# A fused attention and mixture-of-experts kernel on one Trainium2 core: the first pairs' loads and transposes issued in another order, a table load moved forward, and scale and row-half steps moved in VectorE's order

## Chip, cores and metric

The kernel runs on one core of a Trainium2 chip. The metric is the device time of one execution in microseconds (us). A core has five engines with queues of their own: PE (TensorE, matrix products; its weight loads are listed as PEld), DVE (VectorE), ACT (ScalarE), POOL (GpSimd) and SP (SyncE, which here only issues DMAs). DMAs are issued by SP, ACT and POOL; the issuing is listed under SPq, ACTq and POOLq.

## What is computed

Attention over 4 batches, 8 heads, 576 positions, 64 dimensions, in which only scores within `tau` (0.02) of a row's maximum take part, and then a mixture of 8 experts of which each token uses one:

```python
scores = scale * q @ k.T                                   # per batch and head
thresh = max(scores, -1) - tau
scores = where(scores >= thresh, scores, -1e9)
attn   = exp(scores - max); attn /= sum(attn) + 1e-9
x      = (attn @ v), heads side by side                    # 2304 tokens x 512
logits = x @ w_gate; e = argmax(logits); gate = softmax(logits)[e]
# each expert takes at most `capacity` (576) tokens, in token order
h = relu(x[e's tokens] @ w1[e])                            # 512 -> 1024
y = h @ w2[e]                                              # 1024 -> 512
out[token] = gate * y                                      # 0 where not kept
```

All arrays are float32. The kernel splits each operand of a product into a float16 high half and a float16 low half and sums three products.

## The kernel before

**Attention.** The 32 (batch, head) problems are done as 16 pairs of two heads, four pairs to a batch. For pair s the kernel loads k and q (`load`, L730 for the main part, L733 for the two 64-row tails) and v (L728); loads of v for pairs 0 and 1 are issued by POOL. ACT writes the high half (`emit_hi`, L745), DVE the low half for pairs 0 and 1 (`emit_lo`, L754) and POOL that of the later pairs (L752). SP then issues a transposing DMA for k (`emit_turn_k`, L774) and one for q (`emit_turn_q`, L779). PE multiplies kT and qT into scores s (L792), DVE takes the maxima (L819 to L825) and forms from them an additional column block m (`emit_m`, L833 to L838), which a third transposing DMA turns (`emit_turn_m`, L784). PE then computes the differences d = s - max (L792 again, other operands), ACT exponentiates (L880), DVE keeps what is over the threshold (L884), ACT and POOL split p (L850, L854), PE multiplies with v (`av`, L900 and L912), DVE divides (L935), and the result goes through x, logits (L966, L981), gate (L1021 and on) and a scatter of token rows to a buffer `xd` in DRAM, sorted by expert.

**Mixture of experts.** Rows of `xd` are gathered in 21 tiles of 128 tokens: 8 early ones (one for each expert, gathered once three of the four batches are scattered) and 13 late ones (gathered after the last batch). For each tile PE transposes the rows (`x0`, L351), ACT writes the high half (`xh`, L354), DVE the low half (`xl`, L359), PE multiplies with w1 (`A`, L377 for early tiles, L384 for late ones), ACT and DVE make the hidden rows (L402, L406), late ones are transposed by a DMA (L412), PE multiplies with w2 (`B`, L423). The weights come in two chunks of F; their halves are made by ACT (L307, L309, L310), DVE (L314) and POOL (L312). `scales` (L430 and L433) reads two columns of gathered rows and makes the output row numbers `oix` and the factors `gsc`; it runs once for the early tiles and once for each group of 8 late tiles, so it waits until the last gather of its group has landed.

**What sets the order.** The program is not written in execution order. Each step is a task, `T(key, engine, duration, function, dependencies, priority)`, and the class `Plan` (L35 to L163) simulates the engines with a list scheduler: at each moment an engine takes, of the tasks whose dependencies are done, the one with the lowest priority number. The tasks are emitted in the order found, and the semaphore waits follow from the data. A dependency that is only in the plan changes the order on all engines but adds no wait by itself; an engine executes its list strictly in order. Priorities of attention tasks are 9 s plus an offset for each kind; those of early tiles were `NU + PR["early"]` plus 0.284 for each tile. `FIRST_A` (L1168) names the loads that ACT issues in place of SP: by (pair, is it q). The lines of the changed kernel are one higher than here after L706, and two higher behind L1418.

Names in the rows: `kr`, `qr` raw k and q; `kn`, `qn` their halves; `kT`, `qT` the transposed halves; `xd` the scattered rows; `earlyx`, `latex` halves of gathered rows; `earlyy`, `latey` the gathered rows and later the output tiles; `w1b`, `w2b` buffers with halves of weights (also used for d and p in attention); `gp`, `b`, `xo`, `s` are PSUM banks.

## Time and profile before

| what | us |
|---|---|
| runs of the kernel before | 628.80, 628.95, 637.29; median 628.95 |
| the profiled execution, its own time | 626.25 |
| its span in the profile | 624.4 |
| PE busy in it | 556.9 |

The profile is of one execution. Times in it run from the span's start. An idle time is put down to the one that released the engine. The granted clock (PEclk) is that of TensorE as a share of full speed.

### The profile page before, as it was taken

To read this page: it belongs to the slowest core of one execution; us is meant where nothing else is said; L and a number is where in the kernel's file an instruction comes from. 1 tells how busy PE (TensorE), PEld (TensorE's weight loads), DVE (VectorE), ACT (ScalarE), POOL (GpSimd) and SP (SyncE) were. 2 spreads that over 40 slices of the span, in tenths; PEclk is the share of its full clock that TensorE was granted. 3 is DMA by queue.
4 is the path that set the end of the run, shared out by engine and by line. 5 is a ranking of instruction groups with operands and counts; after the bars stand their busy time and mean duration, and the time that the engine had idled before them with its cause. 6 is when DMAs were issued, how large, how long until landed. Compare 5 with 4: busy or idle time off the path is not lost.

```text
span 624.4 us, 15985 instructions
## 1 busy us (share of the span) xinstructions
PE 556.9 (89%) x5990; PEld 378.3 (61%) x5990; DVE 432.3 (69%) x990; ACT 383.3 (61%) x523; POOL 426.9 (68%) x366
## 2 busy tenths in 40 slices
PE   0777999998999999999797895799999999999994
PEld 0234666765667666666566784665775577468652
DVE  4667988878886888886877869444555655555652
ACT  4359888878797688574467643448556645644410
POOL 5327887949887389772768536508788948886774
PEclk9989999989999899998798888989999999999997
DMA  5878777736677367662243845962579519861972
GB/s 152 193 174 166 135 149 138 152 95 156 152 171 137 58 172 133 116 87 49 77 141 99 296 160 157 223 157 77 203 194 220 173 67 222 207 202 61 232 185 100
DMA packets 171181, 94.26 MB, mean 151 GB/s; under 512 B 147027, under 2 KB 159383, under 8 KB 171098
## 3 DMA queue, kind: packets, MB, share of 16 engines
q1 hardware_dynamic: 157450, 50.47, 40.1%
q0 software_dynamic: 12352, 41.80, 20.8%
q8 instruction: 52, 0.85, 0.6%
q10 hardware_dynamic: 1296, 0.89, 0.4%
q14 instruction: 31, 0.25, 0.1%
HBM read 53.25 MB, written 10.24 MB: 102 GB/s over the span
## 4 chain that ended last, share of the span: by engine, by line
PE 60%; DVE 14%; DMA 9%; SPq 5%; ACT 4%; issue 4%; POOL 3%; ACTq 0%; POOLq 0%; DVEq 0%
PE b L384 10%; PE xo L900 9%; PE s L792 8%; PE d L792 7%; PE b L377 7%; PE xo L423 5%; PE gp L423 4%; PE b L423 4%; DVE w2b L884 3%; PE gp L966 2%; DMA out_dram<-latey,oix 2%; PE xo L912 2%; DVE mx L819 2%; SPq L733 2%; DMA qr<-in_q_dram 2%
## 5 line engine op out<-in xcount | busy, mean ns | idle before, releaser
L792 PE MATMUL s<-kT,qT 128*128 128x512 f16 (+2 forms) x576 | 99.5, 310 | 28.8 <-DMA kT<-kn 22.2
L819 DVE TENSOR_REDUCE mx<-s 128x1 f32<-128x512 f32 x144 | 94.4, 679 | 17.4 <-PE s L792 16.6
L792 PE MATMUL d<-qT,kT 128*128 128x512 f16 (+2 forms) x576 | 85.4, 302 | 6.0 <-DVE w2b L884 4.5
L384 PE MATMUL b<-w1b,latex 128*128 (+2 forms) x816 | 79.4, 274 | 5.3 <-DVE latex L359 3.6
L309 ACT ACTIVATE ws<-ws 128x1024 f32<-128x1024 f32 x48 | 50.5, 1051 | 51.1 <-DMA ws<-in_moe_w_dram 51.1
L384 PEld LDWEIGHTS <-latex 128*128 128x128 f16 (+1 forms) x816 | 62.3, 102 | 21.3 <-DVE latex L359 4.8
L792 PEld LDWEIGHTS <-qT 128*128 128x128 f16 (+1 forms) x640 | 39.7, 105 | 57.3 <-issue 25.7
L884 DVE SCALAR_TENSOR_TENSOR w2b<-d,ntau,w2b 128x1024 f32<-128x1024 f32 x56 | 71.0, 1276 | 3.6 <-ACT w2b L880 3.6
L854 POOL TENSOR_TENSOR p<-w2b,p 128x1024 f16<-128x1024 f32 x33 | 70.3, 2135 | 3.2 <-ACT p L850 2.8
L312 POOL TENSOR_TENSOR w2b<-ws,w2b 128x1024 f16<-128x1024 f32 x24 | 51.0, 2137 | 23.0 <-ACT w2b L310 22.8
L792 PEld LDWEIGHTS <-kT 128*128 128x128 f16 (+1 forms) x640 | 37.1, 102 | 47.7 <-issue 28.0
L312 POOL TENSOR_TENSOR w1b<-ws,w1b 128x1024 f16<-128x1024 f32 x24 | 51.3, 2141 | 20.6 <-ACT w1b L310 20.3
L880 ACT ACTIVATE w2b<-d 128x1024 f32<-128x1024 f32 x56 | 56.3, 1019 | 5.5 <-PE d L792 4.7
L900 PEld LDWEIGHTS <-p 128*128 128x128 f16 x1056 | 47.2, 103 | 14.8 <-issue 4.1
L377 PE MATMUL b<-earlyx,w1b 128*128 128x128 f16 x768 | 51.1, 228 | 5.4 <-DVE earlyx L359 5.2
L377 PEld LDWEIGHTS <-w1b 128*128 128x128 f16 x768 | 47.4, 102 | 12.8 <-issue 10.3
L900 PE MATMUL xo<-vH,p 128*128 128x65 f16 x704 | 49.9, 199 | 3.9 <-DVE rc L935 2.6
L423 PEld LDWEIGHTS <-lateh 128*128 128x128 f16 (+1 forms) x408 | 30.8, 103 | 33.6 <-issue 0.4
L296 POOL DMA_DIRECT2D ws<-in_moe_w_dram x50 | 37.3, 750 | 9.7 <-DVE w2b L314 7.3
L900 PE MATMUL xo<-vL,p 128*128 128x64 f16 x352 | 43.9, 197 | 0.0
L850 ACT ACTIVATE p<-w2b 128x1024 f16<-128x1024 f32 x33 | 34.8, 1055 | 6.1 <-DVE w2b L884 5.8
L310 ACT ACTIVATE w2b<-ws 128x1024 f16<-128x1024 f32 x24 | 25.4, 1057 | 20.9 <-PE gp L423 20.2
(231 smaller groups left out, 1225.6 us busy)
## 6 DMA issues: line engine op xcount, KB each, us to landing
ws<-in_moe_w_dram POOLq DMA_DIRECT2D x50, 512.0 KB, 5.1
ws<-in_moe_w_dram SPq DMA_DIRECT2D x14, 512.0 KB, 4.7
kr<-in_k_dram SPq DMA_DIRECT2D x15, 256.0 KB, 2.9
qr<-in_q_dram SPq DMA_DIRECT2D x14, 256.0 KB, 2.9
v<-in_v_dram SPq DMA_DIRECT2D x28, 128.0 KB, 3.2
qr<-in_q_dram ACTq DMA_DIRECT2D x2, 256.0 KB, 4.8
v<-in_v_dram POOLq DMA_DIRECT2D x4, 128.0 KB, 3.3
qT<-qn SPq DMA_TRANSPOSE x32, 4.7
```

Of the source, the lines that this page charges most:

```text
L296: eng.dma_start(out=t, in_=src)
L309: nc.scalar.activation(out=t, in_=t, func=AF.Copy, scale=W_SCALE)
L312: nc.gpsimd.tensor_tensor(out=dst[:, :, 1, :], in0=t, in1=dst[:, :, 0, :], op=ALU.subtract)
L377: nc.tensor.matmul(out=hp[:, f * P:(f + 1) * P], lhsT=wb[0][:, o:o + P], rhs=xT[t][:, xi], start=(d == 0 and z == 0), stop=(d == NB - 1 an ...
L384: nc.tensor.matmul(out=hp[m, 0:FC], lhsT=xT[t][:, xi, m], rhs=wb[0][:, bass.ds(r + (2 * d + wi) * FC, FC)], start=(d == 0 and z == 0), sto ...
L423: nc.tensor.matmul(out=yp[m], lhsT=h[:, o, hi, m], rhs=wb[1][:, bass.ds(r + wi * DM, DM)], start=(z == 0), stop=(z == len(ops) - 1),)
L792: nc.tensor.matmul(out=out, lhsT=l, rhs=r, start=(z == 0), stop=(z == 1), **kw)
L819: V.tensor_reduce(out=m[:, i, 0:1], in_=ps_s[i % 2], axis=AX.X, op=ALU.max)
L854: eng.tensor_tensor(out=p[:, 1], in0=p32_of(s, k), in1=p[:, 0], op=ALU.subtract)
L880: nc.scalar.activation(out=t, in_=d, func=AF.Exp, scale=sc_s)
L884: V.scalar_tensor_tensor(out=t, in0=d, scalar=ntau, in1=t, op0=ALU.is_ge, op1=ALU.mult)
L900: nc.tensor.matmul(out=ps_x[:, j * DV:j * DV + r.shape[-1]], lhsT=l, rhs=r, start=(z == 0), stop=(z == len(ops) - 1))
```

## The change

Seven edits, all in the planner's input or in what stands ahead of it:

1. A one-column `Exp` on ACT (L707 of the changed kernel) from the tile `ones`, ahead of everything else that ACT does. Before, ACT's one table load stands ahead of its first ACTIVATE (L745).
2. `FIRST_A` holds q of pair 0 only; q and k of pair 1 are issued by SP.
3. The loads of pair 2 depend on pair 0's transposes in the plan, those of pair 3 on pair 2's; the load of v for pair 2 depends on the transpose of k of pair 2.
4. The transposes of pair 2 depend on `tm` of pair 0, the transpose of its m block.
5. `scales` of a late group depends on the low half `xl` of the group's last tile too.
6. `scales` of the early tiles gets the priority `NU - 6` in place of `NU + PR["early"] + 20`.
7. `x1` and `x2` (`xh` and `xl`) of the early tiles get `NU - 9 + 0.284 t` in place of `NU + PR["early"] + 0.284 t`.

```diff
--- before.py
+++ after.py
@@ -704,6 +704,7 @@
         xss = [right.tile([P, NJ, D + 1], F32, name=f"xs{i}") for i in range(3)]
         rcs = [right.tile([P, 2, NJ, 1], F32, name=f"rc{i}") for i in range(3)]
 
+        nc.scalar.activation(out=cbuf[0][:, 0:1], in_=ones[:, 0:1], func=AF.Exp, scale=sc_s)
         for i in range(NKN):
             V.memset(kns[i][:, 1, :, D:], 0.0)
             V.memset(kns[i][:, 1, :, D:D + 1], MC)
@@ -1165,7 +1166,7 @@
 
         CUT = 2 * NJ + 3
         FIRST = 2
-        FIRST_A = {(0, True), (1, False), (1, True)}
+        FIRST_A = {(0, True)}
         BY_V = set()
         SI = list(range(2 * NJ)) + [2 * NJ, 2 * NJ + 1, 2 * NJ + 2]
         SD = [432] * (2 * NJ) + [560, 560, 180]
@@ -1177,7 +1178,7 @@
                 n = "q" if is_q else "k"
                 src, raws = (q, qraws) if is_q else (k, kraws)
                 eng, en, occ = (nc.scalar, "A", 460) if (s, is_q) in FIRST_A else (nc.sync, "S", 600)
-                T(("l" + n, s), en, 3 * occ, partial(load, src, raws[s % NRAW], s, eng), last("lo" + n, s - NRAW), u + PR["ld"] + is_q, dma=(728, 90, 90), kind="load")
+                T(("l" + n, s), en, 3 * occ, partial(load, src, raws[s % NRAW], s, eng), last("lo" + n, s - NRAW) + ([("tk", 0), ("tq", 0)] if s == 2 else [("tk", 2), ("tq", 2)] if s == 3 else []), u + PR["ld"] + is_q, dma=(728, 90, 90), kind="load")
                 nat = s - (NQN if is_q else NKN)
                 free = last("tm" if is_q else "tk", nat)
                 got = [("l" + n, s)] + ([("tau",)] if is_q and s == 0 else [])
@@ -1190,10 +1191,10 @@
                 T(("hi" + n, s), "A", 1170, partial(emit_hi, s, is_q, scaled), got + free, u + PR["hi"] + is_q)
                 T(("lo" + n, s), "G" if scaled else "V", 1270 if scaled else 760, partial(emit_lo, s, is_q, scaled), [("hi" + n, s)], u + PR["lo"] + is_q)
                 users = [(m, s - NT, i) for m, c in (("s", CUT), ("d", 6)) for i in range(c)] if s >= NT else []
-                T(("t" + n, s), "S", 0, partial(emit_turn_q if is_q else emit_turn_k, s), [("lo" + n, s)] + users, u + PR["tk"] + is_q, dma=2016, kind="turn")
+                T(("t" + n, s), "S", 0, partial(emit_turn_q if is_q else emit_turn_k, s), [("lo" + n, s)] + users + ([("tm", 0)] if s == 2 else []), u + PR["tk"] + is_q, dma=2016, kind="turn")
             vfree = last("av", s - NV, 2, 0) + last("av", s - NV, 1, NJ - 1)
             ve, vn, vo = (nc.gpsimd, "G", 1255) if s < 2 else (nc.sync, "S", 600)
-            T(("lv", s), vn, 4 * vo, partial(load, v, vts[s % NV], s, ve), vfree, u + PR["lv"], dma=(728, 728, 90, 90), kind="load")
+            T(("lv", s), vn, 4 * vo, partial(load, v, vts[s % NV], s, ve), vfree + ([("tk", 2)] if s == 2 else []), u + PR["lv"], dma=(728, 728, 90, 90), kind="load")
             T(("vs", s), "A", 760, partial(emit_vs, s), [("lv", s)], u + PR["vs"])
             T(("vh", s), "A", 620, partial(emit_vh, s), [("vs", s)] + last("av", s - NVS, 1, NJ - 1), u + PR["vs"] + 1)
             T(("vl", s), "G", 1150, partial(emit_vl, s), [("vh", s)], u + PR["vs"] + 2)
@@ -1367,8 +1368,8 @@
         for t in range(NE, NS, GR):
             m = min(GR, NS - t)
             T(("scales", t // GR), "V", 150, lambda t=t, m=m: scales(gst["late"][:, t - NE:t - NE + m], t, m, tb["bad"][:, t - NE:t - NE + m]),
-              [("gather", t + m - 1), ("bad", 1), ("own",)], at(t - NE + m + PM["sc"]))
-        T(("scales", 0), "V", 150, lambda: scales(gst["rows"], 0, NE, fst[:, 1]), [("gather", t) for t in range(NE)], NU + PR["early"] + 20)
+              [("gather", t + m - 1), ("xl", t + m - 1), ("bad", 1), ("own",)], at(t - NE + m + PM["sc"]))
+        T(("scales", 0), "V", 150, lambda: scales(gst["rows"], 0, NE, fst[:, 1]), [("gather", t) for t in range(NE)], NU - 6)
         def all_av(s):
             return [("av", s, x, j) for x in range(3) for j in (range(NJ) if x < 2 else (0,))]
 
@@ -1415,7 +1416,8 @@
                 for t in range(NS):
                     early = t < NE and c == 0
                     n = NU + PR["early"] + t * PR["ej"] if early and i == 0 else at(pos)
-                    o = (lambda p: n) if early and i == 0 else (lambda p: at(pos + PM[p]))
+                    nx = NU - 9 + t * PR["ej"]
+                    o = (lambda p: nx if p[0] == "x" else n) if early and i == 0 else (lambda p: at(pos + PM[p]))
                     if not (early and i == 0):
                         pos += 2 if ends and (i == 0 and t >= NE + MIX or i and t < NS - NE - MIX) else 1
                     ws = [("w1", i, c, t)] if t < NE else [("w", i, c)]
```

SP's list near the start. First before, from the transposes of pair 1 on (L779 and L774 are the transposes of q and k, L784 that of m; `qT_184` belongs to pair 0, `qT_185` and `kT_182` to pair 1, `qT_186` and `kT_183` to pair 2; `v_170` is pair 2, `kr_173` and `qr_175` are pair 3; the loads of `kr_172` and `qr_174` for pair 2 stand just ahead of these rows):

```order
L779 DMA_TRANSPOSE qT_185<-qn_179 128x18x128
L774 DMA_TRANSPOSE kT_182<-kn_177 128x18x128
L728 DMA v_170<-in_v_dram 128x4x64 x2
L733 DMA v_170<-in_v_dram 64x64 x2
L730 DMA kr_173<-in_k_dram 128x2x256
L733 DMA kr_173<-in_k_dram 64x64 x2
L730 DMA qr_175<-in_q_dram 128x2x256
L733 DMA qr_175<-in_q_dram 64x64 x2
L779 DMA_TRANSPOSE qT_186<-qn_180 128x18x128
L774 DMA_TRANSPOSE kT_183<-kn_176 128x18x128
L784 DMA_TRANSPOSE qT_184<-qn_178 128x9x128
```

and the same engine after the change, from the transposes of pair 0 on (the loads of k for pair 0 and of q and k for pair 1 stand ahead of these rows; `kr_172` and `qr_174` are pair 2):

```order
L780 DMA_TRANSPOSE qT_184<-qn_178 128x18x128
L775 DMA_TRANSPOSE kT_181<-kn_176 128x18x128
L780 DMA_TRANSPOSE qT_185<-qn_179 128x18x128
L775 DMA_TRANSPOSE kT_182<-kn_177 128x18x128
L731 DMA kr_172<-in_k_dram 128x2x256
L734 DMA kr_172<-in_k_dram 64x64 x2
L731 DMA qr_174<-in_q_dram 128x2x256
L734 DMA qr_174<-in_q_dram 64x64 x2
L785 DMA_TRANSPOSE qT_184<-qn_178 128x9x128
L1163 DMA cap_i<-in_moe_capacity_dram 128x2
L1165 DMA wg<-in_moe_w_gate_dram 128x4x8
L1155 DMA xd<-zero 4x1x128
```

Between the two the m transpose of pair 0 (L784, L785 after) has gone from behind the loads of pairs 2 and 3 and the transposes of pair 2 to the place behind the loads of pair 2; v of pair 2, the loads of pair 3 and the transposes of pair 2 have gone behind it.

ACT's list at the start, before (the L730 and L733 rows issue loads, `qn_178` and `kn_176` are pair 0):

```order
L730 DMA qr_174<-in_q_dram 128x2x256
L733 DMA qr_174<-in_q_dram 64x64 x2
L730 DMA qr_175<-in_q_dram 128x2x256
L733 DMA qr_175<-in_q_dram 64x64 x2
L730 DMA kr_173<-in_k_dram 128x2x256
L733 DMA kr_173<-in_k_dram 64x64 x2
L745 ACT_TABLE_LOAD
L745 ACTIVATE qn_178<-qr_174,g_72 128x18x64
```

and after the change:

```order
L707 ACT_TABLE_LOAD
L707 ACTIVATE c_189<-ones 128x1
L731 DMA qr_174<-in_q_dram 128x2x256
L734 DMA qr_174<-in_q_dram 64x64 x2
L746 ACTIVATE qn_178<-qr_174,g_72 128x18x64
L746 ACTIVATE kn_176<-kr_172 128x2x9x64
```

The table load has gone to the head of the list, and one load is issued in place of three.

DVE's list among the late tiles, before (`latex` rows are the low halves of late tiles, one for each tile; `oix` is the step `scales`, here that of the second group of late tiles, `hw` the hidden rows):

```order
L359 SCALAR_TENSOR_TENSOR latex<-b_4870,latex 128x512
L406 SCALAR_TENSOR_TENSOR hw<-b_4871,hw 128x256
L359 SCALAR_TENSOR_TENSOR latex<-b_4869,latex 128x512
L430 SCALAR_TENSOR_TENSOR oix<-bad,latey 128x5
L433 TENSOR_SCALAR gsc<-latey 128x5
L406 SCALAR_TENSOR_TENSOR hw<-b_4872,hw 128x256
L359 SCALAR_TENSOR_TENSOR latex<-b_4870,latex 128x512
L406 SCALAR_TENSOR_TENSOR hw<-b_4873,hw 128x256
L314 SCALAR_TENSOR_TENSOR w2b<-ws,w2b 128x512 x2
L359 SCALAR_TENSOR_TENSOR latex<-b_4869,latex 128x512
```

and after the change, from the same place among the late tiles to the second group's `scales`:

```order
L359 SCALAR_TENSOR_TENSOR latex<-b_4871,latex 128x512
L406 SCALAR_TENSOR_TENSOR hw<-b_4873,hw 128x256
L359 SCALAR_TENSOR_TENSOR latex<-b_4870,latex 128x512
L406 SCALAR_TENSOR_TENSOR hw<-b_4874,hw 128x256
L359 SCALAR_TENSOR_TENSOR latex<-b_4871,latex 128x512
L406 SCALAR_TENSOR_TENSOR hw<-b_4872,hw 128x256
L359 SCALAR_TENSOR_TENSOR latex<-b_4870,latex 128x512
L430 SCALAR_TENSOR_TENSOR oix<-bad,latey 128x5
L433 TENSOR_SCALAR gsc<-latey 128x5
L406 SCALAR_TENSOR_TENSOR hw<-b_4873,hw 128x256
```

`scales` of this group has moved from the middle of the low halves to behind the last of them.

PE's list at the first late tile, before (L351 on `latey` transposes a late tile, L384 multiplies it with w1):

```order
L377 LDWEIGHTS w1b
L377 MATMUL b_4872<-earlyx,w1b 128x128
L351 MATMUL b_4869<-ident,latey 128x128 x4
L591 TENSOR_LOAD exi
L604 TENSOR_LOAD nhi
L351 MATMUL b_4870<-ident,latey 128x128 x4
L384 LDWEIGHTS latex
L591 TENSOR_LOAD exi x2
L384 ISA
L384 MATMUL b_4873<-w1b,latex 128x256
```

and after:

```order
L423 LDWEIGHTS earlyh
L423 MATMUL xo<-w2b,earlyh 128x512
L604 TENSOR_LOAD nhi
L351 MATMUL b_4870<-ident,latey 128x128 x4
L351 MATMUL b_4871<-ident,latey 128x128 x4
L423 LDWEIGHTS earlyh
L591 TENSOR_LOAD exi x3
L423 MATMUL b_4875<-w2b,earlyh 128x512
```

In place of the early tiles' products with w1 (L377) those with w2 (L423, 6 rows a tile) stand directly ahead of the first late tile; all 8 early products with w1 and 8 products of L423 now stand ahead of the first late L384, where it was 8 and 3. Further up in PE's list the first two early products with w1 now stand ahead of the last pair's second half of products with v (L900, L901 after), where all stood behind; and in DVE's list the low halves of all eight early tiles stand ahead of the last softmax maxima of the gate (L1021), where the last two stood behind.

## Rows read from the trace of the kernel before

**Rows 1.** The page: PE busy, and shares by engine of the chain that ended last.

```profile
PE 556.9 (89%) x5990; PEld 378.3 (61%) x5990; DVE 432.3 (69%) x990; ACT 383.3 (61%) x523; POOL 426.9 (68%) x366
...
PE 60%; DVE 14%; DMA 9%; SPq 5%; ACT 4%; issue 4%; POOL 3%; ACTq 0%; POOLq 0%; DVEq 0%
```

**Rows 2.** Windows by stage: us, busy by engine, PEclk, DMA share, GB/s.

```profile
18.00:60.00 42.00, 32.55 (x262) 15.31 (x261) 31.42 (x59) 24.71 (x31) 18.22 (x15) 0.96 0.78 174
60.00:300.00 240.00, 230.76 (x2889) 158.58 (x2889) 198.10 (x471) 185.11 (x266) 178.20 (x145) 0.97 0.63 129
300.00:340.00 40.00, 32.29 (x407) 23.43 (x407) 31.61 (x62) 23.96 (x37) 29.88 (x22) 0.89 0.33 104
340.00:410.00 70.00, 55.53 (x552) 47.50 (x550) 49.50 (x157) 34.97 (x74) 35.90 (x35) 0.87 0.71 206
410.00:607.00 197.00, 196.98 (x1825) 129.40 (x1823) 109.13 (x203) 106.21 (x109) 145.76 (x105) 1.00 0.63 166
```

**Rows 3.** Timeline of the start: start, us, engine, line, operation, names.

```profile
0.82 0.47 ACTq L730 DMA_DIRECT2D qr<-in_q_dram  x1
...
1.74 1.20 SPq L733 DMA_DIRECT2D kr<-in_k_dram  x2
...
5.64 1.12 ACTq L733 DMA_DIRECT2D qr<-in_q_dram  x2
...
6.80 0.60 ACTq L730 DMA_DIRECT2D kr<-in_k_dram  x1
...
7.44 1.14 ACTq L733 DMA_DIRECT2D kr<-in_k_dram  x2
8.68 1.28 ACT L745 ACT_TABLE_LOAD   x1 [8.68 <-DMA qr<-in_q_dram]
...
9.97 1.25 ACT L745 ACTIVATE qn<-qr,g 128x1152 f16<-128x1152 f32 x1
...
12.10 2.00 SPq L779 DMA_TRANSPOSE qT<-qn  x1
...
14.21 2.39 SPq L774 DMA_TRANSPOSE kT<-kn  x1
```

**Rows 4.** The chain that ended last, start of it: start, us, what.

```profile
0.82 4.80 DMA qr<-in_q_dram
...
14.21 4.05 DMA kT<-kn
...
18.31 2.82 PE s L792 x6
```

**Rows 5.** Timeline of DVE, end of the first m block.

```profile
29.12 0.20 DVE L838 SCALAR_TENSOR_TENSOR qn<-qn,gp 128x9 f16<-128x9 f16 x1
```

**Rows 6.** Timeline of SP, transposes of pair 2's k and of m.

```profile
33.39 2.65 SPq L774 DMA_TRANSPOSE kT<-kn  x1
36.15 1.25 SPq L784 DMA_TRANSPOSE qT<-qn  x1
...
46.63 1.31 SPq L784 DMA_TRANSPOSE qT<-qn  x1
...
63.83 1.25 SPq L784 DMA_TRANSPOSE qT<-qn  x1
```

**Rows 7.** Waits of PE from 326 to 412: us in total, times, longest.

```profile
PE b L377 <- DVE earlyx L359: 5.2, 1, 5.2
PE b L384 <- DVE latex L359: 3.6, 1, 3.6
...
PE gp L955 <- ACT w2b L960: 2.2, 2, 1.7
```

**Rows 8.** Timeline of PE: the first late product, and one early product with w2.

```profile
387.48 1.89 PE L384 MATMUL b<-w1b,latex 128*128 x12 [1.15 <-ACT latex L354]
...
417.82 1.47 PE L423 MATMUL b<-w2b,earlyh 128*128 128x512 f16 x6
```

**Rows 9.** Timeline of DVE: the second late group of scales.

```profile
404.06 0.17 DVE L430 SCALAR_TENSOR_TENSOR oix<-bad,latey 128x5 int32<-128x5 f32 x1 [5.33 <-DMA latey<-xd,gix]
```

## The prediction

> **What bounds the kernel now.** I read the page's busy shares first, then PE's windows by stage, then the chain and the waits in the stages where PE is not full. PE is busy for 556.9 us and holds 60% of the chain [rows 1], so PE sets the time, and what can be won is time in which PE has nothing to do. The windows say where that is [rows 2]: from 18 to 60 us PE is busy for 32.55 of 42 (9.5 idle), from 60 to 300 for 230.76 of 240 (9.2 idle in 240), from 300 to 340 for 32.29 of 40 (7.7 idle), from 340 to 410, where attention ends and the experts begin, for 55.53 of 70 (14.5 idle, at a granted clock of 0.87), and from 410 to 607 for 196.98 of 197. Ahead of all that lies the start: the first product begins at 18.31 [rows 4]. So an earlier start is worth its full size only if it holds through two stages, the ramp to 60 and the end of attention; behind 410 PE is full, and whatever is won up to there stays won.
>
> **The start (edits 1 and 2).** ACT first issues three loads and only then computes. The load of q for pair 0 goes out at 0.82 and its main part has landed 4.80 later, at 5.62 [rows 3, 4]. But ACT goes on issuing the tails of q of pair 1 at 5.64 and k of pair 1 at 6.80 and 7.44 (1.14), loads its table at 8.68 (1.28), and begins the high half of q at 9.97 [rows 3]. From there the chain runs through the transpose of q at 12.10, that of k at 14.21, which lands 4.05 later, to PE at 18.31 [rows 3, 4]. After the change the table load comes first: from about 0.8 to 2.1. The load of q goes out then, 1.3 later than now, and lands at 2.1 + 4.8 = 6.9 (estimate). Nothing else is queued on ACT ahead of the high half, so this starts at about 6.9 in place of 9.97: 3.1 earlier. The moved loads are paid by SP: three parts of 0.60 to 1.2 for each of q and k [rows 3], from 2.94 (1.74 + 1.20) to some 8.7 if two parts wait as ACT's did; the first transpose is due at 6.9 + 2.1 = 9.0, so SP is just free. First product: 18.31 - 3.1 = 15.2. From both sides: 0 if SP's queue of loads holds up the transpose by 3, and 4 if ACT issues the load of q while the table still loads, so that q lands up to 1.3 earlier than I count, and SP is free by then. I take 3.1, since every step of it but SP's has a row.
>
> The Trainium skill ("ScalarE: Activation LUTs", section "What ACT_TABLE_LOAD costs") puts a switch at about 1283 ns for the load and 1380 ns more for a drain, 2.66 us in all. This trace shows the load with 1.28 and the first ACTIVATE right behind it at 9.97 [rows 3], with no further gap, so it agrees with the first part alone; with the drain the load of q would go out 1.4 later, the start would gain 1.7, and the sum would be 1.4 smaller.
>
> **The ramp (edits 3 and 4).** The m block of pair 0 is written on DVE by 29.32 [rows 5], but its transpose is issued at 36.15, directly behind that of k of pair 2 (33.39, 2.65), so it waits 6.8 for SP alone [rows 6]; all d products of pair 0 wait for it. After the change the loads of pair 3 and pair 2's transposes stand behind it. With the start's 3.1 the m block is ready at about 26.3, and the transpose goes out then: 9.9 earlier than now. What is late next is pair 2: its loads and transposes are pushed behind. From 26.3 on SP issues the transpose of m (1.25), four short loads, the transposes of k and q of pair 2 (2.65 + 2.0), v of pair 2, k and q of pair 3 (1.74 each by the rows of k [rows 3]) and v of pair 3, which by my count, with about 2.6 for each v (an estimate from four parts of 0.6), comes to 43.2 before the transpose of m of pair 1, which now goes out at 46.63: 3.4 earlier. The third goes out at 63.83 now [rows 6] and at about 57.1 by the same count: 6.7 earlier. PE by then has done less of the other work it would have had, some 1.3 us, and 3.4 and 6.7 bracket what arrives at 60 us. I take 6.6 for the start and ramp together, so 3.5 for the ramp alone. From both sides: 0 (pair 2's scores arrive late and PE waits for them as long as it now waits for d), and 5.5, about what is left of the 9.5 us idle in that window [rows 2] after the waits for maxima and softmax that nothing here touches.
>
> **The end of attention (edits 5 to 7).** Three things count here. First, PE waits 3.6 for a late tile's low half [rows 7]; DVE stands at `scales` of the second late group until 404.06, after 5.33 of waiting for the last gather of that group [rows 9], and the low halves are queued behind it. With edit 5 that step stands behind the last low half, so the 3.6 goes. Second, PE waits 5.2 for the last early low halves [rows 7]. In the new order all early low halves are made ahead of the gate's sums, and 5 further early products with w2 stand ahead of the first late product. Each takes 1.47 [rows 8], or 7.4 us in all, which PE now does behind 410, where it is full. They fit in the 14.5 idle us of the window [rows 2]. Third, what it costs: the first late product, now at 387.48 [rows 8], has 8 products with w2 in front, and DVE makes seven w2 low halves ahead of the first late low half, against some now made later. I count about 4 us of later start for the late tiles. The sum is 3.6 + 7.4 - 4 = 7.0. From both sides: -2 (the late tiles start 11 later and eat more than both gains) and 9 (they don't start later at all, but some of the 14.5 idle must remain for the logits, the gate and the gathers). I take 4.5, nearer to the 3.6 than to the 9: the 3.6 hangs on one list alone, while the 7.4 needs the w2 halves in time, and its rows are of a stretch behind the window, at full clock [rows 2, 8]. Edit 6 costs nothing by itself: two small DVE steps stand earlier, beside PE's early products.
>
> **The sum.** 3.1 + 3.5 + 4.5 = 11.1. Against the profiled execution (626.25) that gives 615.15; that execution is 2.7 under the median of the runs shown, 628.95. From the median: 628.95 - 11.1 = 617.85, so 617.9. A measurement of this kernel can tell about 2% from no change, 12.6 us: the bounds are 616.4 and 641.5.
>
> **Rivals.**
> - *Larger.* The early products with w2 all fall into idle time and the late tiles aren't delayed: 9 in place of 4.5, and the better filled stretch from 340 to 410 also gets back some of the clock; at 0.87 in 55.53 us of busy time [rows 2] full clock would be worth up to 7, half of it 3.5. Then 628.95 - 3.1 - 3.5 - 9 - 3 = 610.4. For it speaks that the idle is there; against it that the gate's chain from logits to gathers isn't shortened.
> - *The end of attention gives nothing.* The list puts early products with w1 ahead of the last pair's products with v, and so the last logits, gate and gathers come later by as much as the fill wins. Only the first two terms hold: 628.95 - 6.6 = 622.4. For it speaks the wait of 2.2 at the last x [rows 7], a chain that any delay of the last pair lengthens.
> - *The ramp gives nothing.* Pair 2's late transposes make PE wait for scores as long as it waited for d: 628.95 - 3.1 - 4.5 = 621.4. For it speaks that SP, not PE, is the queue there [rows 6].
> - *The start doesn't move.* SP, with three pairs of loads, is busy when q is ready, and the transpose of k lands at 18.3 as before: 628.95 - 3.5 - 4.5 = 621.
> - *Slower.* One mechanism: two early products with w1 now stand in PE's list ahead of the last pair's products with v. If their low halves or the w1 halves aren't ready, PE stands there in order, and the last logits, gate, scatter, gathers and first late product are all later by that wait. The price is the wait itself, as the late chain is then the longest. It decides once it exceeds the 11.1 won elsewhere; with 14, as much as all of PE's idle time in that window now [rows 2], the time is 628.95 + 2.9 = 631.9. Against it: PE's largest single wait there now is 5.2 [rows 7].
>
> The Trainium skill also states ("DMA: Bandwidth & Descriptors", section "Issuing engines are not separate DMA queues") that spreading DMAs over issuing engines brings no bandwidth and saves issue time only. By that rule taking two loads from ACT loses nothing in bandwidth, and SP pays for it in issue time, which is the rival on the start; rows of ACT issuing up to 8.58 while q lay landed since 5.62 [rows 3, 4] agree with the part on issue time, and no row here shows the bandwidth.
>
> **How the numbers follow.** Forecast 0.42, larger 0.20, no gain at attention's end 0.17, none in the ramp 0.10, start unmoved 0.06, slower 0.05. About a third of the forecast's own spread lies under 616.4, 0.14, and with the larger case 0.34 are faster by over 2%; the slower case would have to reach 641.5, so 0.03 for it; the rest, 0.63, lies within 2%. The range runs from 608 (4 + 5.5 + 9 + 2.5 of clock = 21) to 629 (the slower case left out but for its beginning).
>
> **What would show it.** In the changed trace the table load is at about 1, the high half of q at 7, the first product at 15.2, the first transpose of m at 26 and the third at 57. DVE has no wait of 5 at `scales`, PE none of 3.6 for a late low half; L423 products lie at 370 to 388; the first late product is at 380 to 388. I am wrong if the stretch from 60 to 300 has more waits for kT or qT than before, if PE's idle from 340 to 410 stays at 14, or if the first late product, less what was won earlier, is more than 7 later.

## The result: no gain, and the profile after

The changed kernel takes 635.55 us (median of 20 runs, 632.25 to 644.52), the kernel before 633.15 beside it (20 runs, 626.05 to 642.66). The ratio is 1.0072 with a 95% interval of 1.0045 to 1.0098: 0.7% or some 4.5 us slower, where 11.1 faster was forecast. The ratios in this document leave out runs more than 1.5% above the fastest of the same kernel; of before that is 8 of 20 here and about half beside some later kernels, of the others fewer, so a ratio can come out too high, and the medians of all runs are given where they say something else. Over all runs the medians here are 2.4 us (0.4%) apart. So the gain that was forecast isn't there; that the changed kernel is slower is less certain, and by how much least of all. The time of before also differs from chip to chip (medians of 626 to 637), so ratios are compared and not times. The profiled execution of the changed kernel took 635.40, its span is 633.7, its mean granted clock 0.940, against 0.959 in the profile of before. The two spans lie 9.3 us apart, more than the medians, since the profiled execution of before took 626.25 where its median is 633.15: part of what the two traces differ by is the execution and not the change.

The page, PE's busy time and the chain's shares, to be read against [rows 1]:

```profile
PE 568.3 (90%) x5990; PEld 383.8 (61%) x5990; DVE 433.8 (68%) x990; ACT 384.2 (61%) x524; POOL 425.2 (67%) x366
...
PE 69%; DVE 9%; DMA 9%; POOL 5%; issue 4%; ACT 3%; SPq 1%; POOLq 0%; DVEq 0%; ACTq 0%; another core or an unknown queue 0%
```

PE executes the same 5990 products, but is busy for 11.4 us longer. The granted clock accounts for that: busy time times mean clock is 534 us in both (556.9 x 0.959, 568.3 x 0.940). Its idle time (span less busy) went from 67.5 to 65.4: the 11 us of idle time that the change was to fill are there, all but 2. The windows by stage, columns as in [rows 2]:

```profile
18.00:60.00 42.00, 34.52 (x326) 17.61 (x325) 33.49 (x71) 25.86 (x32) 19.07 (x15) 0.96 0.70 149
60.00:300.00 240.00, 226.41 (x2716) 155.46 (x2714) 189.85 (x431) 177.84 (x256) 170.73 (x139) 0.94 0.58 126
300.00:340.00 40.00, 36.19 (x460) 24.79 (x457) 31.98 (x83) 24.60 (x37) 29.71 (x23) 0.91 0.34 107
340.00:410.00 70.00, 56.30 (x555) 44.39 (x553) 48.28 (x144) 37.22 (x74) 39.12 (x37) 0.83 0.57 179
410.00:607.00 197.00, 195.31 (x1837) 132.90 (x1838) 112.22 (x214) 109.97 (x118) 141.54 (x102) 0.98 0.66 171
```

From 18 to 60 us PE is busy for 2.0 longer than before, from 300 to 340 for 3.9 longer, but from 60 to 300 for 4.4 less, at a clock of 0.94 where it was 0.97 (2716 products in place of 2889), and from 340 to 410 for only 0.8 longer, at 0.83. The gain of the start can be seen. Behind it stands a loss, in a stretch for which the prediction's sum has no term. Of the gain at the end little can be seen here: PE's idle time from 340 to 410 is 13.7, where it was 14.5 and half of that was to be filled. The start itself (timeline, as [rows 3]):

```profile
0.81 1.28 ACT L707 ACT_TABLE_LOAD   x1 [0.81 <-PEq L1513]
...
1.11 0.49 ACTq L731 DMA_DIRECT2D qr<-in_q_dram  x1
...
2.10 0.20 ACT L707 ACTIVATE c<-ones 128x1 f32<-128x1 f16 x1
...
6.27 1.25 ACT L746 ACTIVATE qn<-qr,g 128x1152 f16<-128x1152 f32 x1 [3.97 <-DMA qr<-in_q_dram]
...
8.41 3.09 SPq L780 DMA_TRANSPOSE qT<-qn  x1
...
11.61 2.47 SPq L775 DMA_TRANSPOSE kT<-kn  x1
```

and the waits of PE up to 60 (as [rows 7]):

```profile
PE s L793 <- DMA kT<-kn: 15.9, 1, 15.9
...
PE s L793 <- DMA qT<-qn: 2.6, 2, 1.6
```

The table loads from 0.81 and q goes out at 1.11, while it loads. The high half begins at 6.27, the transposes at 8.41 and 11.61, the first product at 15.9 (it was 18.31). The m transposes, in the timeline of SP [rows 6]:

```profile
26.99 1.34 SPq L785 DMA_TRANSPOSE qT<-qn  x1
...
45.67 1.33 SPq L785 DMA_TRANSPOSE qT<-qn  x1
...
59.88 1.26 SPq L785 DMA_TRANSPOSE qT<-qn  x1
```

The first is 9.2 earlier, the second 1.0, the third 3.9. The rest of them are in the table below, as a ruler of how far attention has come: row by row the same 16 instructions, one for each pair.

| kernel | 1st | 2nd | 3rd | 5th | 8th | 12th | 16th |
|---|---|---|---|---|---|---|---|
| before | 36.2 | 46.6 | 63.8 | 94.8 | 157.3 | 236.4 | 319.6 |
| changed | 27.0 | 45.7 | 59.9 | 97.3 | 165.5 | 248.9 | 327.7 |
| head_only | 26.7 | 44.8 | 59.1 | 97.8 | 160.3 | 239.3 | 321.8 |
| start_alone | 33.5 | 43.1 | 61.1 | 91.7 | 154.3 | 233.8 | 318.5 |
| ramp_alone | 27.9 | 45.9 | 60.0 | 94.5 | 158.5 | 239.4 | 322.8 |
| m_turn_behind_v | 28.0 | 43.2 | 57.2 | 91.5 | 154.0 | 235.0 | 319.3 |
| middle_only | 34.5 | 44.3 | 61.8 | 99.4 | 168.6 | 250.8 | 327.8 |
| middle_to_pair_7 | 35.0 | 44.8 | 62.0 | 100.0 | 167.9 | 244.3 | 326.8 |
| late_scales_alone | 34.8 | 45.3 | 62.5 | 93.7 | 156.3 | 235.8 | 318.3 |
| early_rows_alone | 35.0 | 45.4 | 62.7 | 93.8 | 157.9 | 237.0 | 319.7 |
| tail_only | 35.0 | 45.4 | 62.8 | 93.9 | 156.4 | 235.5 | 317.7 |

The last three have the lists of before up to pair 14; with before they show the spread of the ruler among executions of the same lists: 1 to 2 us. The changed kernel stands 2.5 behind before at the fifth pair, 8 behind at the eighth and the last.

The ruler compares like with like only where the same lists stand behind. In a re-sorted list an m transpose can stand elsewhere among the same work: at the sixth pair the changed kernel is 2.4 ahead. So here is PE's work itself, that is its busy time times the granted clock, added up over windows of 10 us to the time shown, less that of before (us, rounded):

| kernel | 60 | 100 | 140 | 160 | 260 |
|---|---|---|---|---|---|
| changed | 4 | 3 | 1 | -5 | -9 |
| head_only | 4 | -4 | -3 | -4 | -3 |
| m_turn_behind_v | 4 | 3 | 2 | 3 | -1 |
| middle_only | 1 | 1 | -3 | -9 | -11 |
| tail_only | 0 | 1 | 1 | 1 | 1 |

The changed kernel is 4 ahead at 60 and 3 at 100. It loses 6 between 140 and 160 and 4 more up to 260. What head_only loses between 60 and 100 isn't lost in it. (tail_only has the lists of before up there, so its row shows the spread.)

### The profile page after: what moved, and what is told of

Read it like the earlier page. It is cut to its first block, busy times and chain, and to the rows that moved or that the text cites. A ratio compares the mean times of both kernels' runs of the same rounds, so it can differ in the third digit from the quotient of the medians.

```text
span 633.7 us, 15992 instructions
## 1 busy us (share of the span) xinstructions
PE 568.3 (90%) x5990; PEld 383.8 (61%) x5990; DVE 433.8 (68%) x990; ACT 384.2 (61%) x524; POOL 425.2 (67%) x366
## 4 chain that ended last, share of the span: by engine, by line
PE 69%; DVE 9%; DMA 9%; POOL 5%; issue 4%; ACT 3%; SPq 1%; POOLq 0%; DVEq 0%; ACTq 0%; another core or an unknown queue 0%
PE b L384 11%; PE xo L901 11%; PE s L793 10%; PE d L793 8%; PE b L377 7%; PE gp L423 5%; PE b L423 4%; PE xo L423 4%; DMA qT<-qn 3%; PE gp L967 3%; DMA out_dram<-latey,oix 2%; DVE mx L820 2%; PE xo L913 2%; PE b L351 2%; DVE w2b L885 2%
## 5 line engine op out<-in xcount | busy, mean ns | idle before, releaser
L793 PE MATMUL s<-kT,qT 128*128 128x512 f16 (+2 forms) x576 | 100.6, 312 | 27.1 <-DMA kT<-kn 15.9
L820 DVE TENSOR_REDUCE mx<-s 128x1 f32<-128x512 f32 x144 | 94.5, 681 | 27.7 <-PE s L793 26.7
L384 PE MATMUL b<-w1b,latex 128*128 (+2 forms) x816 | 82.1, 278 | 4.6 <-ACT hw L402 2.9
L384 PEld LDWEIGHTS <-latex 128*128 128x128 f16 (+1 forms) x816 | 63.6, 103 | 21.9 <-issue 5.1
L312 POOL TENSOR_TENSOR w2b<-ws,w2b 128x1024 f16<-128x1024 f32 x24 | 51.0, 2138 | 19.0 <-ACT w2b L310 18.8
L901 PEld LDWEIGHTS <-p 128*128 128x128 f16 x1056 | 48.8, 105 | 17.4 <-issue 8.4
L901 PE MATMUL xo<-vH,p 128*128 128x65 f16 x704 | 51.5, 203 | 4.7 <-DVE rc L936 3.1
L423 PEld LDWEIGHTS <-lateh 128*128 128x128 f16 (+1 forms) x408 | 30.7, 103 | 33.8 <-issue 0.8
L377 PEld LDWEIGHTS <-w1b 128*128 128x128 f16 x768 | 45.4, 100 | 8.2 <-issue 5.8
L377 PE MATMUL b<-earlyx,w1b 128*128 128x128 f16 x768 | 48.6, 223 | 1.5 <-DVE earlyx L359 1.5
L901 PE MATMUL xo<-vL,p 128*128 128x64 f16 x352 | 45.3, 201 | 0.0
L855 POOL TENSOR_TENSOR p<-w1b,p 128x1024 f16<-128x1024 f32 x11 | 23.5, 2135 | 23.7 <-ACT p L851 23.7
L851 ACT ACTIVATE p<-w2b 128x1024 f16<-128x1024 f32 x33 | 34.8, 1053 | 4.9 <-DVE w2b L885 4.4
```

Of the source, the lines that this page charges most:

```text
L312: nc.gpsimd.tensor_tensor(out=dst[:, :, 1, :], in0=t, in1=dst[:, :, 0, :], op=ALU.subtract)
L377: nc.tensor.matmul(out=hp[:, f * P:(f + 1) * P], lhsT=wb[0][:, o:o + P], rhs=xT[t][:, xi], start=(d == 0 and z == 0), stop=(d == NB - 1 an ...
L384: nc.tensor.matmul(out=hp[m, 0:FC], lhsT=xT[t][:, xi, m], rhs=wb[0][:, bass.ds(r + (2 * d + wi) * FC, FC)], start=(d == 0 and z == 0), sto ...
L423: nc.tensor.matmul(out=yp[m], lhsT=h[:, o, hi, m], rhs=wb[1][:, bass.ds(r + wi * DM, DM)], start=(z == 0), stop=(z == len(ops) - 1),)
L793: nc.tensor.matmul(out=out, lhsT=l, rhs=r, start=(z == 0), stop=(z == 1), **kw)
L820: V.tensor_reduce(out=m[:, i, 0:1], in_=ps_s[i % 2], axis=AX.X, op=ALU.max)
```

## The experiments

**How the parts were taken apart.** To undo an edit in the planner's input re-sorts all lists behind it, which would mix the edit with the re-sorting. So in these kernels the planner runs once with the old settings and once with the new ones, and the tasks are emitted in the order of the one up to a named task, and then, the rest, in the order of the other:

```diff
-        plan.run()
+        seen = set()
+        for mode, key in SEGMENTS:
+            plan = build(mode)
+            order = plan.run()
+            until = [r[0] for r in order if r[2] == key] + [float("inf")]
+            part = [r for r in order if r[2] not in seen and r[0] < until[0]]
+            seen |= {r[2] for r in part}
+            plan.emit(part)
```

`OLD` and `NEW` stand for the settings of the two kernels, `None` for the end; d2 and d14 are the first d products of pairs 2 and 14. Lines of these kernels are some 4 or 5 higher in the rows than those of before (the s and d products, L792, are L796 or L797). The `Exp` of edit 1 is in those whose start is new.

**head_only**

```diff
+SEGMENTS = [(NEW, d2), (OLD, None)]
```

> The lists of the changed kernel up to pair 2's d products (some 60 us), then the lists of before. Theory A (the start's gain is real and holds where the later lists stay as they were): pair 0's m transpose at 27 and the third at 60 as in the changed kernel, and the time 4 to 6 us under before (ratio 0.990 to 0.994). Rival B (what the start wins is given back by 80 us, whatever the later lists are): the fifth m transpose is no earlier than in before, and the time is that of before within 2 us.

Measured: ratio 1.0081, 1.0050 to 1.0112. Slower by 5, where theory A had 4 to 6 faster; also more than rival B's 2. The ruler is 9.5 ahead of before at the first pair, 4.8 at the third, and 2 to 3 behind from the fifth on. PE's waits from 55 to 110:

```profile
PE s L797 <- DMA qT<-qn: 4.2, 2, 3.0
PE gp L960 <- ACT w2b L965: 1.3, 1, 1.3
```

and the windows from 60 to 105, of this kernel:

```profile
60.00:105.00 45.00, 39.65 (x448) 25.59 (x446) 32.95 (x63) 34.99 (x50) 30.60 (x25) 0.92 0.68 136
```

and of before:

```profile
60.00:105.00 45.00, 43.95 (x573) 30.07 (x573) 37.94 (x81) 38.16 (x55) 34.76 (x29) 1.00 0.75 144
```

PE is idle for 5.4 of these 45 us and the clock falls to 0.92 (0.66 from 75 to 85, 1.00 in the rest), where before had 1.1 and 1.00. What PE waits for is seen on SP (its timeline; L789 is the m transpose, L779 and L784 those of k and q, here of pair 2 and then of pair 4):

```profile
21.27 1.11 SPq L738 DMA_DIRECT2D qr<-in_q_dram  x2
26.69 1.31 SPq L789 DMA_TRANSPOSE qT<-qn  x1
...
30.38 1.95 SPq L779 DMA_TRANSPOSE kT<-kn  x1
...
67.83 2.00 SPq L779 DMA_TRANSPOSE kT<-kn  x1
...
71.69 2.24 SPq L784 DMA_TRANSPOSE qT<-qn  x1
```

SP has issued the last load at 22.4 and stands at pair 0's m transpose until 26.7. From there to 73.9 it has no pause of over 0.3 us, and the transpose of q of pair 4, issued at 71.7, lands when PE has waited 3.0 for it. In before SP had no such pause between 12 and 59 either, but never stood waiting there, and paused for 4.3 in all between 59 and 66.2: that was its slack. In before the same transpose goes out at 73.3, 1.6 later than here; but PE, which is 4 ahead here at 60, needs it earlier. In the changed kernel it goes out at 68.4, because SP's list there has no loads between the transposes of k and q of pair 4, where the list of before, which follows here, has them; there PE has no wait for it, and the clock is 1.00 from 60 to 100. So by these traces the loss belongs to the joint of the two lists in head_only, and not to the changed kernel.

**middle_only**

```diff
+SEGMENTS = [(OLD, d2), (NEW, d14), (OLD, None)]
```

> The lists of before, but those of the changed kernel between pair 2's and pair 14's d products; nothing of the edits to the start or the end. Theory A (the loss lies in the re-sorted middle of attention, where pairs 6 to 7 took 30.5 us against 22.6): 5 to 8 us slower than before (ratio 1.008 to 1.013). Rival B (those 8 us are a granted clock of 0.87 that one execution happened to have, the lists cost nothing): the time of before within 2 us.

Measured: 1.0103, 1.0068 to 1.0138. Theory A holds, rival B falls: with the old start and the old end the re-sorted middle costs 6.5, and the ruler shows the jump at the same place as in the changed kernel, between the seventh and the eighth pair.

**tail_only**

```diff
+SEGMENTS = [(OLD, d14), (NEW, None)]
```

> The lists of before up to pair 14's d products, then those of the changed kernel, so edits 5 to 7 alone. The prediction's term: 4.5 us faster than before. By the two traces, in which the stretch from the last d product to the end took 295.8 in the changed kernel and 294.6 before: 1 us slower, with the first late gather about 4 later behind the last d product and the first late product with w1 about 4.6 later.

Measured: 0.9913, 0.9879 to 0.9947, or 5.4 faster; the prediction's term of 4.5 was right and my reading of the changed trace (1 slower) wrong. The window from 325 to 420, of this kernel:

```profile
325.00:420.00 95.00, 83.55 (x852) 63.47 (x851) 67.43 (x180) 58.43 (x108) 49.45 (x45) 0.93 0.68 185
```

and of before:

```profile
325.00:420.00 95.00, 76.83 (x811) 63.41 (x809) 65.73 (x178) 50.97 (x101) 48.56 (x43) 0.89 0.65 188
```

PE is busy for 6.7 longer in it, at a higher clock. The late products begin at 388.15 (387.48 before [rows 8]), but then run on: from 385 to 450 PE is idle for 0.3.

**head_and_tail**

```diff
+SEGMENTS = [(NEW, d2), (OLD, d14), (NEW, None)]
```

> The lists of the changed kernel at the start and the end, those of before in the middle. Theory A: the start's gain less the end's loss, 3 to 5 us faster than before. Rival B: the time of before, 0 to 2 us slower.

Measured: 0.9925, 0.9887 to 0.9963. The changed kernel without its middle is faster than before. By the two ratios the middle costs the changed kernel 1.5%, some 9 us. The time is theory A's size, but not by theory A's sum, since head_only is slower and tail_only alone has 5.4. The parts don't add cleanly: head_only and tail_only sum to -0.06%, and -0.75% (-1.13 to -0.37) was measured, while head, middle and tail sum to 0.81 + 1.03 - 0.87 = 0.97%, where the change has 0.72 (0.45 to 0.98). The ruler shows the head's loss here too (98.3 at the fifth pair, 325.6 at the last), so either the tail wins more behind it or one of the ratios is off; that stays open.

**start_alone**

```diff
+SEGMENTS = [(NEW, tm0), (OLD, None)]
```

> Edits 1 and 2 alone: the changed kernel's lists up to pair 0's m transpose, which is left where it was before, behind the loads of pair 3 and the transposes of pair 2; all lists from there as before. The prediction's term: 3.1 us faster; by the changed kernel's trace the first product comes at 15.9 in place of 18.3, 2.4 earlier. Theory D (the start is a plain gain, and the loss at 80 us comes from edits 3 and 4): all m transposes 2 to 2.5 earlier up to the last, 2 to 2.5 us faster. Rival E (an earlier start is lost in any order, since the softmax engines or buffers set the pace up to 100 us): the fifth m transpose no earlier than before, the time of before.

(`tm0` is pair 0's m transpose.) Measured: 1.0044, 0.9995 to 1.0093, and the medians of all runs are 632.2 against 636.9: the time leaves it open. The trace speaks for theory D: the first product is at 15.7, and the ruler is 2.6 to 3.7 ahead of before up to the twelfth pair, 1.0 at the last.

**ramp_alone**

```diff
+SEGMENTS = [(OLD + edits 3 and 4, d2), (OLD, None)]
```

> Edits 3 and 4 alone, without the table load and the moved loads, up to pair 2's d products; all lists from there as before. The prediction's term: 3.5 us faster. Theory D: the first m transpose is 6 or more earlier, but the fifth is 5 or more later than before (PE waits for the transposed q of pair 4 for about 3 us at 77, and the granted clock falls to 0.6 behind that), and the time is 3 to 5 us slower. Rival E: the same loss as in head_only comes about only with the earlier start, so here the time of before within 1.5 us.

Measured: 1.0027, 0.9983 to 1.0071. The first m transpose is 8.2 earlier, and nothing of that is left at the fifth; the last is 3.2 later. The 3.5 of the prediction aren't there. The loss isn't 3 to 5 either: rival E was nearer here, but not in start_alone. Theory D's wait isn't there: from 55 to 110 PE waits only 0.3 for a q, and its longest wait is one of 2.1 for ACT (`gp`, L959).

**late_scales_alone**

```diff
+SEGMENTS = [(OLD, d14), (OLD + edit 5, None)]
```

> Edit 5 alone: only the late groups' scales are moved in DVE's list, no other list is changed. The prediction's term: PE's wait of 3.6 for a late low half and DVE's wait of 5.3 at scales go, 3.6 us faster. Rival F (the late product then waits 3 us for the same gather, since the low halves queued behind scales need that gather or the one before it): less than 1 us faster.

Measured: 0.9976, 0.9916 to 1.0036; between the two expectations. In the trace both waits are gone, that of DVE at scales and that of PE for a low half (0.4 is left of it), but another stands in their place (waits of PE from 325 to 430):

```profile
PE b L388 <- ACT latex L358: 5.5, 1, 5.5
PE b L381 <- DVE earlyx L363: 4.2, 3, 3.6
```

ACT made nothing from 392.7 to 400.7 there, and the trace puts that to no engine of this core ("remote", 8.0). The same wait of ACT near 400 is in ramp_alone (8.1), early_rows_alone (6.6) and m_turn_behind_v_and_tail (6.6), and not in the other ten traces, before and tail_only among them. What edit 5 is worth without this is open.

**early_rows_alone**

```diff
+SEGMENTS = [(OLD, d14), (OLD + edits 6 and 7, None)]
```

> Edits 6 and 7 alone: early scales and early row halves earlier, PE's early products re-sorted, late scales where they were. By the prediction's parts: 7.4 of early products with w2 moved into idle time less 4 of later late tiles, so 3.4 us faster. Rival F: as tail_only was 5 to 6 us faster and edit 5 gives next to nothing, all of it is here: 5 us faster.

Measured: 0.9845, 0.9732 to 0.9958, from only 4 runs (median 627.8, before's 636.9). By the time, the gain at the end is in these two edits. The trace doesn't show it: from 325 to 420 PE is idle for 18.8, as in before (18.2), where tail_only has 11.5; the wait of ACT named above stands in that stretch. So it isn't shown which of the edits 5 to 7 fills the idle time, or whether it takes them together.

**start_and_tail, m_turn_behind_v, m_turn_behind_v_and_tail** ran together.

```diff
+SEGMENTS = [(NEW, tm0), (OLD, d14), (NEW, None)]                        # start_and_tail
+SEGMENTS = [(edits 1 to 4 without v's part of 3, d2), (OLD, None)]             # m_turn_behind_v
+SEGMENTS = [(edits 1 to 4 without v's part of 3, d2), (OLD, d14), (NEW, None)]  # with the tail
```

> Edits 1 and 2 at the start as in start_alone, the lists of before in the middle, edits 5 to 7 at the end. If the two gains add (start 2 to 3 us, end 5 to 6 us): 7 to 9 us faster than before (ratio 0.986 to 0.989) and under every other kernel of this study. If the start's gain is lost in the middle, as start_alone's last m transposes hint: 5 us faster (ratio 0.992).

Measured: 0.9942, 0.9911 to 0.9973, or 3.7 faster; by the medians of all runs 5.9 (625.4 against 631.3). The second expectation is nearer; that the two gains add isn't shown.

> As head_only, but the load of v for pair 2 needn't wait for pair 2's transposed k, so SP issues v of pairs 2 and 3 while the m block of pair 0 is still being made, in place of standing idle from 22.4 to 26.7. Theory G (the ramp's loss is SP standing at the m transpose, with 4.3 us of its queue lost and everything behind it late): the first m transpose within 1.5 of head_only's 26.7, the transpose of q of pair 4 at 68 to 70 in place of 71.7, PE's wait of 3.0 for it gone or under 1, and the time 3 to 5 us under head_only's against the same before. Rival H (any order that puts the m transpose ahead of pair 2's transposes costs as much, since pair 2's and 3's scores then come late): the same wait and the same loss as head_only.

Measured: 0.9991, 0.9950 to 1.0033, so 0.9% under head_only; the medians of all runs are 628.1 and 631.3, 0.5% faster than before. Theory G holds, rival H falls. SP, in the places shown for head_only (L733 is v):

```profile
22.07 1.28 SPq L733 DMA_DIRECT2D v<-in_v_dram  x2
...
24.70 1.28 SPq L733 DMA_DIRECT2D v<-in_v_dram  x2
...
28.03 1.32 SPq L789 DMA_TRANSPOSE qT<-qn  x1
...
70.11 2.17 SPq L784 DMA_TRANSPOSE qT<-qn  x1
```

Two loads of v fill the time in which SP stood still, the m transpose goes out only 1.3 later than in head_only, q of pair 4 1.6 earlier, and PE's wait of 3.0 for it is gone (waits of PE from 55 to 110):

```profile
PE gp L960 <- ACT w2b L965: 1.0, 1, 1.0
PE s L797 <- DVE mx L824: 0.9, 3, 0.5
PE s L797 <- DMA qT<-qn: 0.9, 2, 0.6
```

The clock from 60 to 105 is 1.00 again. The ruler is 3 ahead of before from the fifth pair to the eighth, and level at the last. (Leaving v out of edit 3 also moves other loads and the transposes of pair 3 on SP, so the standing still isn't the only thing that differs from head_only.)

> As m_turn_behind_v, and edits 5 to 7 at the end. Theory G: 6 to 9 us faster than before, level with start_and_tail or under it. Rival H: as head_and_tail was, ratio 0.992 to 0.995.

Measured: 0.9900, 0.9866 to 0.9935: 6.3 faster than before (7.6 by the medians of all runs, 623.7 and 631.3). Of the kernels with over 4 runs it has the lowest ratio, though its interval overlaps those of tail_only and start_and_tail. By the two ratios it is 1.7% under the changed kernel.

**middle_to_pair_7**

```diff
+SEGMENTS = [(OLD, d2), (NEW, d of pair 7), (OLD, None)]
```

> As middle_only, but the lists of the changed kernel stand only between pair 2's and pair 7's d products, so they cover the first batch's gate, where PE in middle_only waited 2.1 at 147.7 for the gate to read the bank that the next transpose of x overwrites, and the granted clock fell to 0.50 behind it. Theory I (middle_only's loss is made there): the eighth m transpose 9 to 12 later than in before, and 5 to 8 us slower (ratio 1.008 to 1.013). Rival J (the loss is spread over all pairs to 14): under 3 us slower.

Measured: 1.0146, 1.0096 to 1.0196. Theory I: this stretch alone has the loss of the middle, and more. PE's waits from 60 to 170 and its windows there:

```profile
PE gp L959 <- DVE tb L1079: 2.1, 1, 2.1
```

```profile
140.00:150.00 10.00, 6.72 (x78) 4.24 (x78) 9.53 (x30) 6.25 (x10) 6.85 (x7) 1.00 0.92 178
150.00:160.00 10.00, 9.69 (x90) 6.46 (x88) 6.36 (x13) 5.83 (x9) 7.73 (x8) 0.66 0.41 103
```

Before, the same windows:

```profile
140.00:150.00 10.00, 8.23 (x115) 5.74 (x114) 9.75 (x22) 7.37 (x13) 8.53 (x9) 1.00 1.01 230
150.00:160.00 10.00, 10.00 (x129) 6.77 (x126) 8.35 (x22) 9.29 (x12) 9.66 (x8) 1.00 0.24 45
```

At the end of batch 0 the list of before puts the gate's last rank product at 139.5 and then, before the next transpose of x uses the bank `gp`, a group of scores and one of differences. In the re-sorted list that rank product stands at 144.3, one group of differences ahead of the transpose, which then waits 2.1 until DVE has read the bank (L1079, `emit_gate2`). PE is busy for 1.5 less from 140 to 150 (idle 3.3 in place of 1.8), and from 150 to 160 the clock is 0.66, in middle_only 0.61, where it was 1.00.

DVE comes to that read late because of the step just ahead of it. It takes 2.71 here, where before has 0.15, and ends together with a step of POOL (timelines of DVE and POOL, of this kernel, and of DVE before):

```profile
144.94 2.71 DVE L1061 TENSOR_TENSOR cum<-cum,oh 64x8 f16<-64x8 f16 x1
145.50 2.13 POOL L858 TENSOR_TENSOR p<-w2b,p 128x1024 f16<-128x1024 f32 x1
```

```profile
140.98 0.15 DVE L1057 TENSOR_TENSOR cum<-cum,oh 64x8 f16<-64x8 f16 x1
```

At 0.15 the read would come at about 145.1, ahead of PE, which is there at 145.7 (an estimate from these rows). In the changed kernel the same step takes 1.77, from 142.74 to 144.51, beside POOL's from 142.37 to 144.49. The same common end is seen at one more DVE step in this kernel (140.10, POOL 140.08) and at one in before (139.06, POOL 139.03), so what holds DVE seems to be POOL's step; no run moved it. The wait and the low clock are there too (waits of PE from 130 to 165 and windows of the changed kernel):

```profile
PE gp L956 <- DVE tb L1076: 2.1, 1, 2.1
```

```profile
140.00:150.00 10.00, 6.81 (x79) 5.14 (x78) 7.13 (x20) 6.85 (x12) 8.01 (x7) 0.71 1.23 252
150.00:160.00 10.00, 10.00 (x113) 6.91 (x112) 7.07 (x12) 5.69 (x8) 6.16 (x8) 0.78 0.07 17
```

From 140 to 160 the mean clock is 0.74 in the changed kernel and in middle_only, 0.83 in this one, and 1.00 in the other eleven traces, none of which has the re-sorted lists there.

## Why the prediction was wrong, step by step

The step that failed is the middle. Between the forecast (11.1 faster) and the ratio (some 4.5 slower) lie 15.6 us. By the ratios of the changed kernel and of head_and_tail the middle is some 9 of them; the rest, some 6, is what start, ramp and end fall short of 11.1 in head_and_tail (4.7 by its ratio).

- *The start.* Forecast 3.1, first product at 15.2; measured 2.4, at 15.9. Right but for size: q went out and landed sooner than I counted (high half at 6.27, counted 6.9), as in the upper bound, but SP's transpose of q then took 3.09, where [rows 3] had 2.00, and that of k went out at 11.6, counted 11.1. Over all traces the gain is smaller still: the first product lies at 17.4 to 18.3 in the seven with the old start and at 15.4 to 16.5 in the seven with the new one, 1.7 apart in the mean. The gain stays until the twelfth pair where nothing else is changed (start_alone). The drain of the Trainium skill's page "ScalarE: Activation LUTs" (section "What ACT_TABLE_LOAD costs") cost nothing here: q was issued at 1.11, during the load, and the 0.20 us ACTIVATE ran at 2.10, right behind it.
- *The ramp.* Forecast 3.5, so 6.6 with the start; in the changed kernel PE's work is 4 ahead at 60 and 3 at 100. So the two terms are there, but too large by about 2.6 to 3.6. I took the m transposes' issue times as the measure of what PE gains, and they came as counted for the first (27.0, counted 26.3) and less so for the others (45.7 and 59.9, counted 43.2 and 57.1). Edit 4 also puts a wait at the head of SP's list, and I priced only the pushing back of pair 2, not the 4.3 us in which SP issues nothing. That costs where the list of before follows: in head_only q of pair 4 then comes too late for PE, and the lead of 4 at 60 is a lag of 4 at 100. That the order on SP, and not the earlier m block, makes this loss is shown by m_turn_behind_v. In the changed kernel PE doesn't wait there. The rival "the ramp gives nothing" named the right queue for head_only, and was given 0.10.
- *The middle.* The prediction's sum has no term for it. That an earlier start only had to hold "through two stages, the ramp to 60 and the end of attention" assumed that the lists between them stay as they are, though the change re-sorts every list from pair 2 on. In place of nothing the runs show 6.5 (middle_only) to 9 (changed kernel against head_and_tail), and by middle_to_pair_7 it is made by pair 7. PE's work in the changed kernel goes from 1 ahead at 140 to 5 behind at 160; 4 more go by 260, and where is open. That a bank's reader comes late to PE's next use of the bank, held by a DVE step of 1.77 to 2.71 us, is what the traces show at that place. A list with that one product moved wasn't run, so how much of the loss is this wait, how much the clock behind it (0.74 for 20 us in the changed kernel, worth some 5) and how much the rest is read from the traces alone. Nor is it shown that the wait brings the clock down: in before PE waits 1.8 for another step at 143.4, and the clock stays at 1.00.
- *The end.* Forecast 4.5; measured 5.4 (tail_only). The size is right, in part by luck: I took the 3.6 of edit 5 as sure and the early products as doubtful, and by the times edit 5 alone gives some 1.5, which its interval can't tell from nothing, and edits 6 and 7 alone, from 4 runs, more than the 5.4. In the changed kernel DVE's wait at `scales` and PE's of 3.6 for a low half are gone, as forecast, and the first late product comes 4.6 later behind the last m transpose than before (counted 4), but 12.75 later in all, at 400.23 (named were 380 to 388). The stretch from the last pair's d products to the end took 1 us longer than before, at a clock of 0.83 from 340 to 410. The sign that I had named, PE's idle time there staying at 14, came: 13.7. A part of what the end wins was thus lost again in that one profile, and why the clock was lower there than in tail_only is open.
- *The range* ended at 629 with a slower rival at attention's end. A slower case by re-sorting wasn't among the rivals.

## What to carry to other kernels

Where an order comes from a list scheduler, an edit is not local: price the re-sorted rest as a term of its own, by splicing the old lists behind the new ones, before a gain is put down to the edit. But look at the joint first: a loss there can belong to the two lists meeting, as in head_only, and the trace of the unspliced kernel tells. A wait put earlier into a queue that issues in order, as SP's list here, holds up everything behind it even when its own transfer becomes early; give the queue something that is ready to issue first, as the loads of v here. And compare work done (busy time times granted clock), since marks such as the m transposes move within a re-sorted list.

## What the runs showed that I had not expected

- ACT issued a DMA at 1.11 while its table load ran from 0.81 to 2.09: the load did not hold up ACT's DMA issue. The DMA also stands behind the one-column ACTIVATE in ACT's list, and that ran at 2.10. So what an engine issues and what it executes don't follow each other strictly in the order of the list. I had counted the issue at 2.1, with this as the upper bound only.
- Waits of PE of 2 to 3 us were followed by low-clock stretches at the same places in several kernels: 0.92 from 60 to 105 in head_only and head_and_tail, 0.74 to 0.83 from 140 to 160 in the changed kernel, middle_only and middle_to_pair_7. In those stretches products take up to 1.8 times as long (s products of two, 0.59 us, take 1.06). But such stretches also come without a wait (before has 0.66 from 125 to 130, with PE busy throughout), so what brings them on isn't shown.
- ACT stood still for 6.6 to 8.1 us near 400 in four kernels, with a releaser that the trace can't name.
